# A block-sparse attention and MLP kernel: the fixed keys read by one wide product per head

## The chip, the cores and the metric

One core of a Trainium2 chip runs the whole program. The metric is the device time of one execution in microseconds (us). TensorE (PE) multiplies and writes to PSUM; VectorE (DVE), ScalarE (ACT) and GpSimd (POOL) do the rest of the arithmetic, and SyncE (SP), POOL and ACT issue DMAs.

## The reference

Attention over 4 batches, 8 heads, 768 positions of 64, in blocks of 32 (24 blocks). A query block sees the first and the last block, its neighbours (itself and one to each side), and three sampled blocks; the first and the last query block see everything. The output goes through an MLP with a squared ReLU (512 to 2048 to 512).

```python
mask = np.abs(blk_i - blk_j) <= window          # window = 1
mask = mask | (blk_i == 0) | (blk_j == 0) | (blk_i == n_blocks - 1) | (blk_j == n_blocks - 1)
for qb in range(n_blocks):
    for kb in sampled_blocks[qb]:
        mask[qb * block:(qb + 1) * block, kb * block:(kb + 1) * block] = True
scores = np.where(mask, scale * np.matmul(q, k.transpose(0, 1, 3, 2)), -1000000000.0)
attn = softmax(scores)                          # max, exp, sum + 1e-09
x = np.matmul(attn, v)                          # heads side by side: 3072 x 512
h = np.maximum(x @ w_in, 0.0)
return (h * h @ w_out)
```

## The kernel before

**Attention.** 128 query positions (4 blocks, index `j`) are a tile `t`; each batch `b` has 6, 24 in all, counted `k` in `order`. Half of the heads (4, as two pairs; `u` is the half, `i` the pair, `e` the head in the pair) of one tile is a `Half`, 48 in all. A pair's two heads lie on partitions 0 to 63 and 64 to 127. A Half's scores are two PSUM banks, one for each `e`; a pair takes 256 columns there: 64 for the two fixed blocks, 96 sampled, 96 neighbours (the window). Every block row `j` has its own sampled keys, so each product takes 32 queries: its shape on the array is 64 rows by 32 columns. Two products make a row of scores: one of 96 columns from `kn`, the batch's keys in block order, and one of 160 from `KG`, a tile into which the fixed keys are copied (four times, once for each `j`) beside the sampled ones. `static_keys` makes these copies, on POOL in the first batch and on ScalarE for the first two tiles of each later batch.

Then: maxima (DVE), exps (ACT), a turn of the probabilities (transposes `pt` on PE with copies `pT` in the first tiles; from tile 6 on ACT and DVE alone), and the values: per head and `j`, one product with V tile 0 (rows 0 to 63 the fixed blocks, 64 to 127 two sampled ones) and one with V tile 1 (rows 0 to 31 the third sampled block, 32 to 127 the window), 128 rows by 32 columns each, `pv`. `norm` divides. The first and last query blocks of a batch, which see everything, are four `Whole`s per batch (`g`, `pg`, `ptg`, `pvg`).

**MLP.** Three tiles make a chunk `c` of 384 positions, 8 chunks. `hidden` (`ph`) and `project` (`po`) each take three reduced-precision products for one exact one; in chunk 0 `project` uses plain fp32. Weights come raw from memory (`craw`) and are cut to fp32 by ACT and DVE (`cut`, `cut_bits`, `cut_split`), `AHEAD` steps behind the load. Attention of chunk c + 1 and later is woven into the MLP of chunk c by `Stream`, a list of generators with hand-set lags (`LAG`, `LAG_1`).

**The start.** Chunk 0's attention has no MLP to hide behind. Its four Wholes and six Halves begin `STEP_0` rounds apart, each with the lags of `LAG_0`. In it ACT also spreads the fixed values over the tiles (`copy_static`), ACT, POOL and DVE copy the windows of tiles 1 and 2 from `vn` (`copy_window`, one half of the heads at a time), and every `CUT_0[1]` rounds a weight cut begins. The SP queue brings tile 0's windows, then for each of the tiles 0, 1, 2 its twelve sampled blocks (`load_sampled`), whose addresses come from registers. Each engine works strictly in the order of the code.

Of the kernel before, what the change touches and what calls it, by code (L numbers as in the profile page):

```python
# [23 lines left out]
BLK = 32  # L24
# [29 lines left out]
AHEAD = 5  # L54
# [27 lines left out]
FIXED_0 = 7  # L82
ON_ACT = 12
# [13 lines left out]
def tile_block_sparse_attention_moe(ctx: ExitStack, tc, kd, knd, qd, qgd, vd, vnd, samp, const, wcat, out):  # L97
# [17 lines left out]
    def bank(name):  # L115
        return ps.tile([P, 512], F32, tag="s", name=name)

# [41 lines left out]
    KG = [one.tile([P, NJ, 2 + NRAND, NPAIR, BLK], F32, name=f"KG{i}") for i in range(2)]  # L159
# [12 lines left out]
    def load_keys(b, u, eng=nc.sync):  # L172

        kn = rot.tile([P, NBLK, 2, BLK], F32, tag=f"kn{u}", name=f"kn{b}_{u}", bufs=1)
        eng.dma_start(kn.rearrange("p a b c -> p (a b c)"), knd[b, u])
        st["kn", b, u] = kn
# [18 lines left out]
    def load_static(k, u, eng=nc.sync):  # L195
        us = halves(k, u)
        if us is None:
            return
        n = 1 if k == 0 else NJ
        for i in range(us.start, us.stop):  # L200
            src = columns(vd[order[k][0], V_STATIC * BLK :], i)
            src = src.unsqueeze(1).broadcast_to([2 * BLK, n, HW // 2])
            eng.dma_start(values_of(k)[0][0 : 2 * BLK, i, 0:n], src)

    def copy_static(k, i, copy):

        src = V[0][0][0 : 2 * BLK, i, 0:1]
        dst = V[k][0][0 : 2 * BLK, i, 1 if k == 0 else 0 :]
        copy(dst, src.broadcast_to(list(dst.shape)))  # L209

    def copy_window(k, i, j, n, copy):
# [5 lines left out]
        copy(V[k][1][(1 + n) * BLK : (2 + n) * BLK, i, j], st["vn", b, i][r : r + BLK, blk // NJ])  # L217

    def load_vn(b, hf, eng=nc.sync, own=None):

        vn = (own or rot).tile([P, NT, HW // 2], F32, tag="vn", name=f"vn{b}_{hf}", bufs=1)
        eng.dma_start(vn.rearrange("p t c -> p (t c)"), vnd[b, hf])
        st["vn", b, hf] = vn
# [15 lines left out]
    def load_q(b, t, eng=nc.sync, own=None):  # L239
        q = (own or rot).tile([P, NJ, NPAIR, BLK], F32, tag="q", name=f"q{b}_{t}", bufs=1 if own else 2)  # L240
# [4 lines left out]
    def keys_of(b, t, own):  # L245
# [3 lines left out]
            own.tile([P, NJ, 2 + NRAND, NPAIR, BLK], F32, name=f"KG{k}") if own else KG[(k - (k >= UC)) % 2]  # L249
# [3 lines left out]
    def copy_keys(b, t, own=None):  # L253

        vals = sampled(t, 0, POOL)
        kg = keys_of(b, t, own)
        for u in range(2):
            if t < UC:
                static_keys(b, t, u, nc.gpsimd.tensor_copy)
            kn = st["kn", b, u]  # L260
            for j in range(NJ):
                for r in range(NRAND):
                    nc.gpsimd.tensor_copy(
                        kg[:, j, 2 + r, 2 * u : 2 * u + 2].unsqueeze(1), kn[:, bass.ds(vals[NRAND * j + r], 1)]
# [5 lines left out]
    def load_kg(b, t):  # L270
# [3 lines left out]
        for j in range(NJ):  # L274
            for r in range(NRAND):
                nc.sync.dma_start(
                    kg[:, j, 2 + r].rearrange("p b c -> p (b c)").unsqueeze(1), k4[:, bass.ds(vals[NRAND * j + r], 1), :]
                )

    def static_keys(b, t, u, copy=nc.scalar.copy):  # L280

        src = st["kn", b, u][:, 0 : NBLK : NBLK - 1].rearrange("p i a c -> p i (a c)").unsqueeze(1)
        dst = st["kg", b, t][:, :, 0:2, 2 * u : 2 * u + 2].rearrange("p j i a c -> p j i (a c)")
        copy(dst, src.broadcast_to(list(dst.shape)))

    def load_window(k, u, eng=nc.sync):
        us = halves(k, u)
        if us is None:
            return
# [34 lines left out]
    class Half:  # L324
# [8 lines left out]
        def run(self, bank, lag):  # L333
# [9 lines left out]
            else:  # L343
                yield lag["x"]
                self.exps()
                self.next_keys()
# [12 lines left out]
        def scores(self):  # L359
# [3 lines left out]
            for i in range(2):  # L363
                pr = 2 * u + i
                for piece in range(2):
                    for j in range(NJ):
                        c = centre(NJ * t + j)
                        for e in range(2):
# [3 lines left out]
                            else:  # L372
                                k, a, z = kg[r, j, :, pr, :], 0, S_WIN
                            nc.tensor.matmul(  # L374
                                self.sb[e][j * BLK : (j + 1) * BLK, i * NSLOT + a : i * NSLOT + z],
                                q[r, j, pr, :],
# [21 lines left out]
        def next_keys(self):  # L398

            b, t = order[min(self.k + self.u, len(order) - 1)]  # L400
            if b > 0 and t < 2:
                static_keys(b, t, 1 - self.u)

        def turn_blocks(self):
# [4 lines left out]
            for j in range(NJ):  # L409
                if j == 2:  # L410
                    self.next_keys()
# [6 lines left out]
            nc.vector.transpose(self.pT.rearrange("p j h c q -> p (j h c q)"), p.rearrange("p j x s -> p (j x s)"))  # L418

# [20 lines left out]
        def copies(self, pt):  # L440
            self.pT = rot.tile([P, NJ, 4, 2, BLK], F32, tag="pT", name=f"pT{self.name}", bufs=2)
            for e in range(2):
                src = pt[e].rearrange("p (h j q) -> p h j q", h=4, j=NJ)
                dst = self.pT[:, :, 2 * e : 2 * e + 2].rearrange("p j i c q -> p (i c) j q")
# [5 lines left out]
        def values(self, bank):  # L450
            po = bank(f"pv{self.name}")
            for i in range(2):
                for e in range(2):
                    h = 2 * i + e
                    hv = h * VW
                    for c in range(2):
                        v = values_of(self.k)[c]
                        for j in range(NJ):
                            nc.tensor.matmul(  # L459
                                po[j * BLK : (j + 1) * BLK, h * VW : (h + 1) * VW],  # L460
                                self.pT[:, j, 2 * e + i, c],
# [544 lines left out]
```

## Time and profile before

| | us |
|---|---|
| median of 3 runs | 760.67 (758.05 to 761.56) |
| profiled execution | 760.55 |
| its span | 758.8 |
| PE busy | 732.4 (97%) |
| ACT busy | 539.7 (71%) |
| DVE busy | 499.8 (66%) |
| POOL busy | 502.3 (66%) |
| first MLP product (`ph`) begins at | 59.64 |

Spans on an engine are from start to modelled end; matmuls are pipelined, so neighbouring rows overlap, and the distance of two starts says what a row cost. An fp32 product has two records. In rows of PE, 64*32 behind the names is the part of the array used, rows by columns; 64x96 behind it the rows and columns that stream through.

### The profile page before, as it was taken

Reading aid. Unit: us, or ns where it says so; the run is one execution under the profiler, and the core shown is the slowest. Engines: PE = TensorE matmul, PEld = TensorE weight load, DVE = VectorE, ACT = ScalarE, POOL = GpSimd, SP = SyncE. Lnnn points to the kernel's source line nnn. Section 1 sums busy time; section 2 is a strip of 40 time slices with the busy share of each in tenths; the row PEclk is TensorE's granted clock in tenths of the full one; section 3 lists DMA queues with packets and bytes.
Section 4 is the critical chain, followed back from the end, with each engine's and each line's share of the span. In section 5 each row is a group of like instructions: output and inputs, shape, how many; then the busy total and the mean of one; then the engine's idle time right before and its main releaser. Section 6 shows DMA issues by size and latency. Waiting matters only on the chain.

```text
span 758.8 us, 26292 instructions
## 1 busy us (share of the span) xinstructions
PE 732.4 (97%) x9832; PEld 612.3 (81%) x9832; DVE 499.8 (66%) x987; ACT 539.7 (71%) x1193; POOL 502.3 (66%) x636
## 2 busy tenths in 40 slices
PE   4879999999999999999999999999999999999997
PEld 2656776668888888888888888887888888888986
DVE  5785785658785756667777575666868666645452
ACT  5896877798876876789786767679876776733222
POOL 6963844227776675757767567666876575777885
PEclk9799999999999999999999999999999999999999
DMA  8776799544543536544434344655344352201001
GB/s 283 224 215 172 228 264 344 130 117 131 140 114 93 146 86 176 153 109 128 113 105 106 101 126 109 221 120 140 79 124 118 75 143 64 51 1 44 1 1 41
DMA packets 92290, 97.45 MB, mean 128 GB/s; under 512 B 14787, under 2 KB 79428, under 8 KB 92164
## 3 DMA queue, kind: packets, MB, share of 16 engines
q1 hardware_dynamic: 86036, 72.41, 37.1%
q0 software_dynamic: 5696, 22.58, 9.2%
q8 instruction: 78, 1.28, 0.7%
q10 hardware_dynamic: 432, 0.79, 0.3%
q14 instruction: 48, 0.39, 0.2%
HBM read 89.43 MB, written 6.29 MB: 126 GB/s over the span
## 4 chain that ended last, share of the span: by engine, by line
PE 85%; ACT 5%; DMA 4%; DVE 4%; issue 1%; SPq 1%; ACTq 0%; POOL 0%; DVEq 0%; POOLq 0%
PE ph L788 33%; PE po L826 30%; PE s L374 7%; PE pv L459 5%; PE po L816 4%; PE g L546 2%; PE pvg L604 2%; DMA V<-in_v_dram 2%; DMA KG<-in_k_dram 1%; PE xt L773 1%; PE pt L437 1%; DVE xl L777 1%; ACT V L209 1%; DMA kn<-in_kn_dram 1%; SPq L317 1%
## 5 line engine op out<-in xcount | busy, mean ns | idle before, releaser
L413 ACT ACTIVATE pm<-p 32x256 f32<-32x256 f32 x576 | 239.2, 415 | 13.2 <-DVE p L391 4.8
L788 PE MATMUL ph<-xh,wi 128*128 128x384 f32 x832 | 237.8, 347 | 0.0
L826 PE MATMUL po<-wo,gh 128*128 128x512 f32 x672 | 213.8, 399 | 0.0
L755 POOL TENSOR_TENSOR wi<-W,wi 128x512 fp32r<-128x512 f32 x104 | 142.3, 1368 | 68.4 <-DVE wi L754 35.2
L806 POOL TENSOR_TENSOR gl<-gf,gh 128x384 fp32r<-128x384 f32 x112 | 117.4, 1048 | 93.0 <-DVE gf L804 80.6
L755 POOL TENSOR_TENSOR wo<-WO,wo 128x512 fp32r<-128x512 f32 x112 | 145.9, 1302 | 49.5 <-DVE wo L754 48.5
L792 ACT ACTIVATE r<-ph 128x384 f32<-128x384 f32 x128 | 63.0, 492 | 161.3 <-PE ph L788 156.1
L804 DVE SCALAR_TENSOR_TENSOR gf<-ph,r 128x384 f32<-128x384 f32 x112 | 62.3, 556 | 150.3 <-ACT r L792 136.4
L788 PEld LDWEIGHTS ph<-xh,wi 128*128 128x128 f32 x832 | 150.4, 188 | 13.4 <-issue 7.4
L826 PEld LDWEIGHTS po<-wo,gh 128*128 128x128 f32 x672 | 123.5, 188 | 23.0 <-issue 2.8
L788 PE MATMUL ph<-xl,wi 128*128 128x384 f32 x416 | 141.4, 340 | 0.0
L826 PE MATMUL po<-wo,gl 128*128 128x512 f32 x336 | 133.2, 396 | 0.0
L754 DVE CAST wo<-WO 128x512 fp32r<-128x512 f32 x112 | 84.4, 753 | 0.0
L788 PEld LDWEIGHTS ph<-xl,wi 128*128 128x128 f32 x416 | 78.2, 188 | 6.9 <-issue 2.9
L826 PEld LDWEIGHTS po<-wo,gl 128*128 128x128 f32 x336 | 63.1, 188 | 15.7 <-POOL gl L806 1.0
L385 DVE TENSOR_REDUCE m<-s 128x2 f32<-128x512 f32 x96 | 61.6, 683 | 11.2 <-PE s L374 10.9
L799 ACT ACTIVATE gh<-r 128x384 fp32r<-128x384 f32 x112 | 59.0, 526 | 9.3 <-ACT r L792 0.4
L459 PEld LDWEIGHTS pv<-V,pT 128*32 128x32 f32 x3072 | 47.7, 110 | 19.8 <-issue 9.5
L459 PE MATMUL pv<-V,pT 128*32 128x65 f32 x3072 | 56.2, 223 | 5.0 <-ACT pT L446 4.8
L788 PE MATMUL ph<-xh,WI 128*128 128x384 f32 x192 | 54.4, 344 | 0.8 <-ACT xh L776 0.8
L374 PE MATMUL s<-KG,q 64*32 64x160 f32 x1536 | 51.2, 305 | 1.4 <-issue 1.0
L418 DVE STREAM_TRANSPOSE pT<-pm 128x1024 f32<-128x1024 f32 x36 | 44.6, 1239 | 4.9 <-ACT pm L413 4.7
(85 smaller groups left out, 933.0 us busy)
## 6 DMA issues: line engine op xcount, KB each, us to landing
craw<-in_w_dram POOLq DMA_DIRECT2D x32, 512.0 KB, 5.9
V<-in_v_dram SPq DMA_DIRECT2D x504, 32.5 KB, 1.8
KG<-in_k_dram SPq DMA_DIRECT2D x216, 64.0 KB, 2.0
V<-in_v_dram SPq DMA_DIRECT2D x28, 390.0 KB, 4.5
q<-in_q_dram SPq DMA_DIRECT2D x24, 256.0 KB, 3.0
out_dram<-ot SPq DMA_DIRECT2D x21, 256.0 KB, 2.5
V<-in_v_dram SPq DMA_DIRECT2D x16, 292.5 KB, 4.2
vn<-in_vn_dram SPq DMA_DIRECT2D x5, 780.0 KB, 6.4
```

The lines of the kernel that those rows point to most:

```text
L374: nc.tensor.matmul(self.sb[e][j * BLK : (j + 1) * BLK, i * NSLOT + a : i * NSLOT + z], q[r, j, pr, :], k, start=True, stop=True,)
L385: nc.vector.tensor_reduce(m[:, e], self.sb[e].rearrange("p (i c) -> p i c", i=2), axis=AX, op=ALU.max)
L413: nc.scalar.activation(p[a * BLK : (a + 1) * BLK, j], x[j * BLK : (j + 1) * BLK, :, a], AF.Exp, scale=SCALE)
L459: nc.tensor.matmul(po[j * BLK : (j + 1) * BLK, h * VW : (h + 1) * VW], self.pT[:, j, 2 * e + i, c], v[:, self.u, j, hv : hv + VW], start=( ...
L754: nc.vector.tensor_copy(w[:, 0], src)
L755: nc.gpsimd.tensor_tensor(w[:, 1], src, w[:, 0], op=ALU.subtract)
L788: nc.tensor.matmul(ph[:, :TOK], w, x, start=(i == 0), stop=(i == len(steps) - 1))
L792: nc.scalar.activation(r, ph[:, :TOK], AF.Relu)
L799: nc.scalar.activation(gh, r, AF.Square)
L804: nc.vector.scalar_tensor_tensor(gf, ph[:, :TOK], 0.0, r, op0=ALU.max, op1=ALU.mult)
L806: nc.gpsimd.tensor_tensor(gl, gf, gh, op=ALU.subtract)
L826: nc.tensor.matmul(acc[c][u], g[:, at], w[:, k], start=(f == 0 and i == 0), stop=(f == NF - 1 and i == 2))
```

## The change

- **Scores, all batches.** Fixed keys aren't copied any more. For each pair and head, one product with all 128 queries of the tile (64 rows by 128 columns of the array) reads the first and last block of `KN` and gives the 64 fixed columns. The product with `KG` shrinks from 160 to 96 columns. The query's layout in memory and on chip is changed so that a pair's 128 queries are contiguous.
- **Values of the first three tiles.** The fixed blocks have one tile, `fixed`, for which each head has one product with 128 queries (64 rows by 128 columns); V tile 0 is then used from row 64 on (64 rows by 32 columns). Heads alternate in order so that equal shapes meet. `copy_static` is gone; tile 3 loads its fixed blocks four-fold from memory. `pv` and `pvg` of the first batch take their banks from the other PSUM pool.
- **Windows.** Tile 1's are copied for both halves at once, eight on POOL and four on ACT; tile 2's are loaded from memory, ahead of its sampled blocks on the SP queue.
- **Sampled keys of the first batch** are copied for both halves at once, but for tile 0.
- **Order of the start.** Half (0, 0) comes behind the second Whole, units begin 4 rounds apart instead of 5, with other lags; weight cuts are 4 steps behind their loads instead of 5.

```diff
-AHEAD = 5
+AHEAD = 4
-STEP_0 = 5
+N_0 = 1
+STEP_0 = 4
+FROM_MEMORY = (2,)
-LAG_0 = {"s": 2, "x": 2, "t": 3, "c": 2, "v0": 2, "n": 2}
+LAG_0 = {"s": 3, "x": 2, "t": 3, "c": 1, "v0": 3, "n": 2}
-FIXED_0 = 7
-ON_ACT = 12
+FIXED_0 = 22
+ON_POOL, ON_DVE = 8, 0
...
         def scores(self):
...
             for i in range(2):
                 pr = 2 * u + i
+                for e in range(2):
+                    r = slice(e * D, (e + 1) * D)
+                    to = self.sb[e][:, i * NSLOT : i * NSLOT + S_RAND]
+                    nc.tensor.matmul(to, q[r, pr].rearrange("p j s -> p (j s)"), kn[r, 0 : NBLK : NBLK - 1, i, :], start=True, stop=True)
                 for piece in range(2):
...
-                                k, a, z = kg[r, j, :, pr, :], 0, S_WIN
+                                k, a, z = kg[r, j, :, pr, :], S_RAND, S_WIN
...
+            for e, i, at in heads:
+                h = e, i, at
+                if e:
+                    self.products(po, h, 0, VA, 2 * BLK, True, False)
+                    self.products(po, h, 1, VB, 0, False, False)
+                p = self.pT[0 : 2 * BLK, 2 * e + i, 0].rearrange("p j q -> p (j q)")
+                nc.tensor.matmul(po[:, at], p, st["fixed"][:, self.u, at], start=e == 0, stop=e == 1)
+                if e == 0:
+                    self.products(po, h, 1, VB, 0, False, False)
+                    self.products(po, h, 0, VA, 2 * BLK, False, True)
...
-            return [(i * STEP_0, u) for i, u in enumerate(wholes + halves)]
+            whole = wholes[:2] + halves[:N_0] + wholes[2:] + halves[N_0:]
+            return [(i * STEP_0, u) for i, u in enumerate(whole)]
...
+    windows = [(copy_window, k, j, n) for k in range(1, UC) if k not in FROM_MEMORY for j in range(NJ) for n in range(3)]
+    for f, *at in windows[:ON_POOL]:
+        f(*at, nc.gpsimd.tensor_copy)
+    moves, fixed = windows[ON_POOL : ON_POOL + ON_DVE], windows[ON_POOL + ON_DVE :]
```

On PE, the first Half's scores (s) before, where they follow the Wholes' scores (g), values (pvg) and transposes (ptg):

```order
L546 MATMUL g_3_1_536<-kn_1_135,QG 128x256
L604 MATMUL pvg_1_540<-vn_0_133,pTg_1_528 32x65 x24
L584 MATMUL ptg_2_0_566<-ident,pg_2_531 128x128 x4
L584 MATMUL ptg_2_1_567<-ident,pg_2_531 128x128 x2
L374 MATMUL s_0_0_0_595<-kn_0_126,q_0_129 32x96
L374 MATMUL s_0_0_1_596<-kn_0_126,q_0_129 32x96
```

The same on PE in the change; the last two numbers are output partitions and columns, so 128x64 is the wide product:

```order
L581 MATMUL ptg_0_0_419<-ident,pg_0_411 128x128 x4
L581 MATMUL ptg_0_1_420<-ident,pg_0_411 128x128 x2
L353 MATMUL s_0_0_0_427<-KN,q_0_131 128x64
L353 MATMUL s_0_0_1_428<-KN,q_0_131 128x64
L363 MATMUL s_0_0_0_427<-KN,q_0_131 32x96
L363 MATMUL s_0_0_1_428<-KN,q_0_131 32x96
```

The scores begin with one wide product for each of the two heads (and do so again for the second pair), and the first Half's now follow the first Whole's transposes instead of the third's.

On PE, the end of the first Half's values before (pv, the second V tile last), with the transposes (pt) and scores behind it:

```order
L459 MATMUL pv_0_0_868<-V_78,pT_0_0_815 32x65 x4
L459 MATMUL pv_0_0_868<-V_79,pT_0_0_815 32x65 x4
L437 MATMUL pt_0_1_0_906<-ident,p_0_1_799 128x128 x4
L437 MATMUL pt_0_1_1_907<-ident,p_0_1_799 128x128 x4
L374 MATMUL s_1_1_0_984<-kn_1_135,q_1_143 32x96
```

On PE, the beginning of the same values in the change:

```order
L543 MATMUL g_3_0_569<-KN,QG 128x512
L543 MATMUL g_3_1_570<-KN,QG 128x256
L447 MATMUL pv_0_0_591<-fixed,pT_0_0_573 128x65
L457 MATMUL pv_0_0_591<-V_79,pT_0_0_573 32x65 x4
L457 MATMUL pv_0_0_591<-V_78,pT_0_0_573 32x65 x8
L457 MATMUL pv_0_0_591<-V_79,pT_0_0_573 32x65 x4
L447 MATMUL pv_0_0_591<-fixed,pT_0_0_573 128x65 x2
```

The first Half's values moved ahead of the third Whole's transposes, and three shapes take turns in them: fixed, V tile 1 (V_79), V tile 0 from row 64 (V_78).

On ACT, the beginning of the program before (pg are a Whole's exps, pTg its turned copy, L209 the fixed values, L217 the windows):

```order
L562 ACTIVATE pg_0_443<-g_0_0_434,mg_0_438 128x512
L562 ACTIVATE pg_0_443<-g_0_1_435,mg_0_438 128x256
L209 COPY V_78<-V_78 64x780 x2
L209 COPY V_122<-V_78 64x1040
L592 COPY pTg_0_466<-ptg_0_0_451 128x512
L562 ACTIVATE pg_1_469<-g_1_0_446,mg_1_459 128x512
L562 ACTIVATE pg_1_469<-g_1_1_447,mg_1_459 128x256
L209 COPY V_122<-V_78 64x1040
L209 COPY V_124<-V_78 64x1040 x2
L217 COPY V_125<-vn_0_133 32x260 x2
L592 COPY pTg_1_528<-ptg_1_0_504 128x512
```

On ACT, the same stretch in the change:

```order
L559 ACTIVATE pg_0_411<-g_0_0_398,mg_0_402 128x512
L559 ACTIVATE pg_0_411<-g_0_1_399,mg_0_402 128x256
L589 COPY pTg_0_465<-ptg_0_0_419 128x512
L559 ACTIVATE pg_1_468<-g_1_0_407,mg_1_414 128x512
L559 ACTIVATE pg_1_468<-g_1_1_408,mg_1_414 128x256
L589 COPY pTg_1_513<-ptg_1_0_501 128x512
L405 ACTIVATE p_0_0_474<-s_0_0_0_427,m_0_0_471 128x256 x2
L405 ACTIVATE p_0_0_474<-s_0_0_1_428,m_0_0_471 128x256 x2
L428 COPY pT_0_0_573<-pt_0_0_0_559 128x512
L428 COPY pT_0_0_573<-pt_0_0_1_560 128x512
L559 ACTIVATE pg_2_576<-g_2_0_509,mg_2_529 128x512
```

The copies of fixed values and windows are gone from it, and the first Half's exps (p) and copies (pT) stand ahead of the third Whole's exps.

More of the change, by code (lines that the diff above doesn't have):

```diff
@@ L158, in tile_block_sparse_attention_moe @@
     W1 = {f: one.tile([P, DM], F32, name=f"W1{f}") for f in SINGLE}
-    KG = [one.tile([P, NJ, 2 + NRAND, NPAIR, BLK], F32, name=f"KG{i}") for i in range(2)]
+    KN = one.tile([P, 2, NBLK, 2 * BLK], F32, name="KN")
+    KG = [one.tile([P, NJ, NRAND, NPAIR, BLK], F32, name=f"KG{i}") for i in range(2)]
     WO = {f: one.tile([P, DM], F32, name=f"WO{f}") for f in range(WO_LOW)}
@@ L195, in load_static, with copy_window @@
     def load_static(k, u, eng=nc.sync):
[L196 to L211, printed above, removed]
+        src = columns(vd[order[k][0], V_STATIC * BLK :], u)
+        src = src.unsqueeze(1).broadcast_to([2 * BLK, NJ, HW // 2])
+        eng.dma_start(values_of(k)[0][0 : 2 * BLK, u], src)
+    def copy_window(k, j, n, copy):
         b, t = order[k]
@@ L255, in copy_keys @@
         vals = sampled(t, 0, POOL)
[L256 to L260, printed above, removed]
+        k5 = keys_of(b, t, own).rearrange("p j r (u a) c -> p j r u (a c)", u=2)
+        for us in (slice(0, 1), slice(1, 2)) if t == 0 else (slice(0, 2),):
             for j in range(NJ):
@@ L396, in maxima @@
                 )
[L398 to L402, printed above, removed]
         def turn_blocks(self):
@@ L598, in values @@
             vn = st["vn", b, pr // 2]
-            po = bank(f"pvg{self.name}")
+            po = (ONE if self.b == 0 else bank)(f"pvg{self.name}")
             for kt in range(NT):
@@ L890, in tile_block_sparse_attention_moe @@
     load_q(0, 2, own=begin)
+    for k in FROM_MEMORY:
+        load_window(k, None)
     load_sampled(2, 1, nc.sync, SP)
-    windows = {
-        (k, u): [(copy_window, k, u, j, n) for j in range(NJ) for n in range(3)] for k in range(1, UC) for u in range(2)
-    }
     for k in range(2):
```

99 lines of the change are left out of this document (47 added, 52 removed).

## The prediction

> **What bounds the kernel now.** I read the page first (busy time, the slices), then the busy time by stage, then TensorE's rows in one steady stage and in the start.
>
> ```profile
> span 758.8 us, 26292 instructions
> PE 732.4 (97%) x9832; PEld 612.3 (81%) x9832; DVE 499.8 (66%) x987; ACT 539.7 (71%) x1193; POOL 502.3 (66%) x636
> ```
> ```profile
> 20.00:30.00 10.00, 7.80 (x270) 6.12 (x261) 7.53 (x24) 9.72 (x24) 9.44 (x26) 0.84 0.94 300
> 30.00:40.00 10.00, 8.93 (x238) 7.02 (x237) 8.52 (x24) 7.89 (x18) 10.00 (x42) 0.66 0.66 172
> 40.00:50.00 10.00, 7.90 (x320) 6.36 (x320) 8.27 (x17) 9.91 (x22) 2.83 (x9) 1.00 0.67 183
> 50.00:60.00 10.00, 6.82 (x169) 5.50 (x157) 7.89 (x20) 9.71 (x20) 7.53 (x25) 1.00 0.97 272
> 160.00:300.00 140.00, 140.00 (x2022) 118.76 (x2020) 98.03 (x197) 108.99 (x252) 94.49 (x95) 1.00 0.48 120
> ```
>
> Behind stretch and length each row has the busy time of TensorE, its weight loads, VectorE, ScalarE and GpSimd, then TensorE's granted clock, the DMA share and GB/s. There are two regimes. From about 60 us on TensorE is never free (140.00 of 140.00 at clock 1.00): there a microsecond that TensorE gains or loses is one of the whole, and what ScalarE, VectorE or GpSimd save is worth nothing. Up to 60 us ScalarE is the full one (9.71 to 9.91 of 10 in three of the four stretches), while TensorE has gaps. The change takes work from ScalarE in the start, and gives TensorE other work in both regimes. So the question is what TensorE pays.
>
> **The scores, where TensorE is full.** These are TensorE's rows around one half's values (pv) and scores (s) in mid-kernel; the tile after the operand names is rows*columns of the array, and an fp32 product has two records.
>
> ```profile
> 211.45 0.40 PE L826 MATMUL po<-wo,gl 128*128 128x512 f32 x1
> 211.78 0.89 PE L604 MATMUL pvg<-vn,pTg 128*32 128x65 f32 x48
> 212.59 0.73 PE L826 MATMUL po<-wo,gh 128*128 128x512 f32 x2
> 213.16 0.39 PE L826 MATMUL po<-wo,gl 128*128 128x512 f32 x1
> 213.39 0.63 PE L826 MATMUL po<-wo,gh 128*128 128x512 f32 x2
> ...
> 214.19 1.12 PE L459 MATMUL pv<-V,pT 128*32 128x65 f32 x64
> 215.23 0.40 PE L374 MATMUL s<-kn,q 64*32 64x96 f32 x16
> 215.42 0.48 PE L374 MATMUL s<-KG,q 64*32 64x160 f32 x16
> 215.69 0.37 PE L374 MATMUL s<-kn,q 64*32 64x96 f32 x16
> 215.86 0.58 PE L374 MATMUL s<-KG,q 64*32 64x160 f32 x16
> 216.37 0.44 PE L788 MATMUL ph<-xh,wi 128*128 128x384 f32 x1
> 216.65 0.34 PE L788 MATMUL ph<-xl,wi 128*128 128x384 f32 x1
> 216.83 0.51 PE L788 MATMUL ph<-xh,wi 128*128 128x384 f32 x2
> ```
>
> Read starts, not durations, which overlap. Sixteen KG records of 160 columns run from 215.42 to 215.69: 0.27 us, and eight tiles work side by side. Cutting 160 to 96 frees 0.27 x 64/160 = 0.108 per pair, 0.22 per half. The wide products put the same 64 columns through tiles of 64x128, of which only two (the two heads) fit side by side. One record of 160 columns takes 0.27/2 = 0.135 of its tile, so 64 take 0.054, two records 0.108, both heads together 0.108 per pair. That is what was freed: **as streaming, the exchange is even.** It can't gain.
>
> What is new is the change of tile shape in mid-stretch. What such a change costs stands in these rows. From pv (128*32) to s (64*32): 65 columns need 0.054 a record, 64 records four abreast 0.87, so pv's stream ends at 215.06 and s starts at 215.23: 0.17. From 128*128 to 128*32: one po record takes 0.23 (213.16 to 213.39), so the one of 211.45 ends at 211.68 and pvg starts at 211.78: 0.10. Back from 128*32 to 128*128: 48 records take 0.65, to 212.43, the next starts at 212.59: 0.16, and its first two take 0.57 against 0.47: 0.10 more for weights that weren't loaded ahead, 0.26 in all. From 64*32 to 128*128: 216.13 to 216.37 is 0.24, and 0.28 against 0.18 for the first record: 0.34. kn to KG, 64*32 both, costs nothing.
>
> Each half after the change goes wide, narrow, wide, narrow. Beside before, that is two changes to narrower columns, one back to wider, and wide weights at the entry. No row has 64*128, so the price is bounded: 0 if the two shapes share the array; at most 2 x 0.17 + 0.34 + 0.10 + 0.2 for weights of second records = 0.98. The nearest rows are those in which only the columns change: 2 x 0.10 + 0.26 + 0.10 = **0.56 us a half**, which I take. The halves of tiles 3 to 23 are computed while TensorE is full: 21 x 2 = 42. 42 x 0.56 = **+23.5 us** (0 to 41).
>
> The Trainium skill's page "TensorEngine Tiling (Array Packing)", Key Properties, speaks against the change: going to another tiling mode, not merely to another tile, empties the array first. The 0.17 and 0.26 agree; for 64x128 no run here shows it yet. By the rule the term is the 23.5, without it 0. Its page "TensorE: Matmul & The Clock Gate", LDWEIGHTS, has a weight load last as long as its columns, about 107 ns for 128. By that an estimate is that two loads a head, 0.21 a pair, outlast the streaming of 0.108, another 0.2 a half, and the whole would be 800.
>
> **The start.** The rows by ScalarE line from 10 to 60 us, the loads of tile 0's sampled values (all twelve, then the last two), and rows of the kinds that are counted below:
>
> ```profile
> L217 ACT COPY V<-vn 32x260 f32<-32x260 f32 x24 | 9.7, 406 | 0.4
> L423 ACT ACTIVATE p<-s,m 128x256 f32<-128x256 f32 x24 | 9.7, 530 | 0.1
> L446 ACT COPY pT<-pt 128x512 f32<-128x512 f32 x12 | 7.0, 662 | 2.0 <-PE pt L437 1.9
> L209 ACT COPY V<-V 64x1040 f32<-64x1040 f32 (+1 forms) x6 | 5.5, 987 | 0.0
> L710 ACT ACTIVATE craw<-craw,below 128x512 int32<-128x512 uint16 x6 | 5.2, 873 | 0.0
> L562 ACT ACTIVATE pg<-g,mg 128x512 f32<-128x512 f32 (+1 forms) x8 | 4.2, 578 | 8.4 <-DVE mg L555 8.4
> ```
> ```profile
> L317 SPq DMA_DIRECT2D V<-in_v_dram x12: 569/570/702, 8.2 to 20.7; - x12
> ...
> DMA to landing us min/median/max: 2.2/5.3/9.8
> ```
> ```profile
> L317 SPq DMA_DIRECT2D V<-in_v_dram x2: 569/570/570, 20.0 to 20.7; - x2
> ...
> DMA to landing us min/median/max: 4.8/5.3/5.9
> ```
> ```profile
> 24.83 0.87 PE L584 MATMUL ptg<-ident,pg 128*128 128x128 f32 x6
> ...
> 34.94 1.96 PE L459 MATMUL pv<-V,pT 128*32 128x65 f32 x64
> ...
> 53.97 1.09 PE L437 MATMUL pt<-ident,p 128*128 128x128 f32 x8
> ...
> 55.21 1.25 ACT L446 COPY pT<-pt 128x512 f32<-128x512 f32 x2
> ...
> 57.34 1.53 PE L773 MATMUL xt<-ident,x 128*128 128x128 f32 x12
> 59.64 0.44 PE L788 MATMUL ph<-xh,WI 128*128 128x384 f32 x1 [0.78 <-ACT xh L776]
> ```
>
> ScalarE loses the six static value copies (5.5) and 24 window copies (9.7), gets four window copies of twice the width (about 0.6 each, between L217's 0.41 and L209's 0.99: 2.4) and one weight cut fewer (about 1.6): 14.4 us less. That would be the gain, were ScalarE still last. Two things take its place.
>
> First, the values of half (0,0) move up in TensorE's order, from behind all four Wholes to behind two. In the chain g, exps, ptg, s, exps, pt, copies they could start near 20 us. But they read the sampled values of tile 0, the twelve loads whose last is issued at 20.7 and lands 5.9 later, at **26.6**; before, they began at 34.94 and never waited. The change leaves those twelve on the SP queue behind the same loads (one fewer). Everything on TensorE behind this product waits too: ptg of Wholes 2 and 3, all later scores; and behind them ScalarE's copies.
>
> Second, TensorE itself. A half's values were 1.04 in steady rows. Now the fixed blocks have a product of their own per head (64 rows x 128 columns, 65 through: 0.108, four times 0.43), and shapes go 64*128, 128*32, 64*32, 128*32 and back twice: 3 x 0.17 + 0.26 = 0.77, twice 1.54. 1.04 + 0.43 + 1.54 = 3.0 (1.5 to 3.5). Scores are 1.14 (215.23 to 216.37) + 0.56 = 1.7. From 26.6 the order holds six pv (18.0), five s (8.5), five pt (5.4), two ptg (1.7), two pvg (1.8): 35.4. In the last two halves nothing lies between pt and pv, so the copies are waited for: 2 x 1.25. From the last pv's end to the first ph before: 57.34 to 59.64, 2.3. Sum 26.6 + 35.4 + 2.5 + 2.3 = 66.8, against 59.64: **+7.2 us**. Per half ScalarE needs 1.62 of exps and 1.17 of copies (9.7 and 7.0 over six) and 1.6 for a cut (0.87 and its like), 4.4 against TensorE's 5.8, so it is covered. If shapes are free, pv is 1.5 and ScalarE is last: behind the first pv it has two pTg copies (1.2), one Whole's exps (1.05), the window copies (2.4), a cast (0.7) and five times 4.4: 27.3; the last cut (1.6) doesn't delay. Then 26.6 + pv 1.5 + ptg 0.9 + 25.7 + pv 1.5 + 2.3 = 58.5: -1.1. Low end: besides that the last load lands 2.2 after issue, at 22.9: -4.8. High: +10, and more if the granted clock falls to the 0.66 of 30 to 40 us.
>
> **The rest.** The static key copies, six on GpSimd in the start and twelve on ScalarE under the full TensorE, and merged key copies: 0, since both engines have room there (GpSimd waits for tile 0's keys and is ready before the first scores). Tile 2's windows by DMA (0.8 MB), and four-fold static values of tile 3 (0.4 MB more): 1.2 MB at 270 GB/s are 4.4 us of transfers, at 40 to 50 us, where the DMA share is 0.67; tile 2's sampled loads move about 1 us later, and its values come far later than that. Without this cover 1 to 2 us. One step less of lead for raw weights: 0 to 2, taken as 0. The flat layouts of q and pT: 0. The bank that pv takes elsewhere frees pt: at most one pT copy, within the low end.
>
> Sum: 760.55 (this execution, 758.8 of span; the median is 760.67) + 23.5 + 7.2 = **791 us**.
>
> **Rivals.** (1) *Shapes share the array.* Then scores cost 0 and the start -1.1, giving 759.4. For it: tiles of one shape do run eight abreast. Against it: every change of shape in these rows has a gap. (2) *Faster*: the same, and the sampled values land at 22.9, since the first raw weights are asked for at another time: 755.7. It decides only if a half's scores pay under 0.05 us, since 42 x 0.05 is 2. (3) *Half price*: only the return to wide costs, 0.26 a half: +11, start +2: 773.
>
> **Numbers.** A difference under 0.5% (3.8 us) can't be told from none. Forecast 0.65 (775 to 808: from 0.36 a half, 15 in all, and no loss in the start, to 0.9 a half and +10); half price 0.09, slower too; shapes free and no change 0.09; faster 0.17. So slower 0.74, same 0.09, faster 0.17. The range must reach past rival 1 to hold 8 in 10: 757 to 808.
>
> **What would show it.** Right: gaps of 0.1 to 0.3 in TensorE's starts around each 64*128 row, and about 1.7 from a half's first score to the next ph; span in the full stage longer by 0.5 to 0.6 a half; the first pv waiting for a DMA near 26 us; the first ph near 67. Wrong: a stretch of 1.14 as before, or a first ph before 58. The forecast fails if 64*128 and 64*32 follow each other without a gap.

## The result, and the profile after

The change makes the kernel slower: 801.4 us (median of 4 runs, 798.07 to 805.04) against 759.79 (4 runs, 758.05 to 761.56), a ratio of 1.054 with a 95% interval of 1.050 to 1.059. The runs of the changed kernel differ with their mean granted clock (0.972 to 0.985); the profiled one is the longest, 805.04, with a span of 803.3. So its span grew by 44.5, from 758.8. Two kernels below, the one without the early half and the one with the filled wait, had one execution of four in a slower state, over 1.5% above their fastest, and their times are those of the other three.

The busy time by stage of the changed kernel, with the columns as before (stretch, length, TensorE, its weight loads, VectorE, ScalarE, GpSimd, TensorE's granted clock, DMA share, GB/s):

```profile
20.00:30.00 10.00, 2.84 (x36) 1.76 (x37) 1.44 (x4) 0.25 (x1) 7.79 (x21) 0.69 0.87 273
30.00:40.00 10.00, 10.00 (x172) 7.61 (x171) 3.08 (x8) 4.39 (x8) 2.89 (x12) 0.50 0.70 170
40.00:50.00 10.00, 10.00 (x284) 7.90 (x284) 7.00 (x23) 5.96 (x15) 3.88 (x14) 0.96 0.53 123
50.00:60.00 10.00, 8.18 (x217) 6.15 (x222) 3.75 (x9) 7.46 (x17) 0.41 (x1) 0.90 0.70 175
60.00:70.00 10.00, 10.00 (x142) 7.34 (x126) 4.81 (x10) 3.29 (x8) 2.43 (x4) 0.50 0.88 239
70.00:80.00 10.00, 10.00 (x121) 7.51 (x121) 2.82 (x8) 2.94 (x5) 0.00 (x0) 0.50 0.24 58
160.00:300.00 140.00, 140.00 (x1848) 114.24 (x1847) 94.58 (x188) 107.98 (x247) 81.84 (x90) 1.00 0.47 120
```

In the start the bound has moved. ScalarE, full before (9.7 to 9.9 of 10), now has room everywhere; TensorE stands idle from 20 to 28 us but for a few products, and from then on it is the full engine, but for some 36 us at half clock. In the full stage nothing is idle, as before. TensorE's rows in the start (duration behind the start; in brackets the idle time ahead and what ended it) say how long the start became:

```profile
19.87 0.40 PE L447 MATMUL pv<-fixed,pT 64*128 64x65 f32 x2
20.20 0.51 PE L457 MATMUL pv<-V,pT 128*32 128x65 f32 x4
26.02 0.43 PE L457 MATMUL pv<-V,pT 128*32 128x65 f32 x2 [5.31 <-DMA V<-in_v_dram]
28.30 1.39 PE L457 MATMUL pv<-V,pT 128*32 128x65 f32 x26 [1.85 <-DMA V<-in_v_dram]
...
45.71 0.43 PE L447 MATMUL pv<-fixed,pT 64*128 64x65 f32 x2
...
48.75 1.09 PE L419 MATMUL pt<-ident,p 128*128 128x128 f32 x8
...
58.11 0.38 PE L363 MATMUL s<-KN,q 64*32 64x96 f32 x4 [1.82 <-issue]
...
60.34 0.68 PE L447 MATMUL pv<-fixed,pT 64*128 64x65 f32 x2
...
65.29 1.97 PE L419 MATMUL pt<-ident,p 128*128 128x128 f32 x8
...
82.48 0.45 PE L786 MATMUL ph<-xh,WI 128*128 128x384 f32 x1 [0.67 <-ACT xh L774]
```

The first MLP product comes at 82.48 instead of 59.64: 22.8 us of the 44.5. The other 21.7 lie behind it. One half in mid-kernel:

```profile
227.21 1.12 PE L457 MATMUL pv<-V,pT 128*32 128x65 f32 x64
228.25 0.44 PE L353 MATMUL s<-KN,q 64*128 64x64 f32 x4
228.62 0.40 PE L363 MATMUL s<-KN,q 64*32 64x96 f32 x16
228.81 0.37 PE L363 MATMUL s<-KG,q 64*32 64x96 f32 x16
229.11 0.44 PE L353 MATMUL s<-KN,q 64*128 64x64 f32 x4
229.48 0.40 PE L363 MATMUL s<-KN,q 64*32 64x96 f32 x16
229.67 0.37 PE L363 MATMUL s<-KG,q 64*32 64x96 f32 x16
229.97 0.45 PE L786 MATMUL ph<-xh,wi 128*128 128x384 f32 x1
```

From the first score to the next product it takes 1.72 us (228.25 to 229.97), where it took 1.14. All halves between 100 and 700 us have this as their median.

### The profile page after: what moved, and what is told of

Its sections match the earlier page's. It is cut to its first block, busy times and chain, and to the rows that moved or that the text cites. A ratio compares the mean times of both kernels' runs of the same rounds, so it can differ in the third digit from the quotient of the medians.

```text
span 803.3 us, 26982 instructions
## 1 busy us (share of the span) xinstructions
PE 782.0 (97%) x10264; PEld 648.1 (81%) x10264; DVE 494.4 (62%) x975; ACT 520.0 (65%) x1155; POOL 484.0 (60%) x566
## 4 chain that ended last, share of the span: by engine, by line
PE 92%; DMA 2%; DVE 2%; ACT 1%; SPq 1%; issue 1%; POOL 0%; ACTq 0%; POOLq 0%; DVEq 0%
PE ph L786 33%; PE po L824 28%; PE pv L457 7%; PE s L363 6%; PE po L814 5%; PE s L353 4%; PE g L543 2%; DMA q<-in_q_dram 2%; PE pt L419 2%; PE pvg L601 2%; PE pv L447 1%; PE xt L771 1%; DMA V<-in_v_dram 1%; DVE xl L775 1%; PE ptg L581 0%
## 5 line engine op out<-in xcount | busy, mean ns | idle before, releaser
L752 DVE CAST wo<-WO 128x512 fp32r<-128x512 f32 x112 | 81.6, 729 | 0.0
L457 PE MATMUL pv<-V,pT 128*32 128x65 f32 (+1 forms) x3072 | 62.8, 229 | 7.2 <-DMA V<-in_v_dram 7.2
L457 PEld LDWEIGHTS pv<-V,pT 128*32 128x32 f32 (+1 forms) x3072 | 49.3, 112 | 24.9 <-issue 11.8
L380 DVE TENSOR_TENSOR p<-s,m 128x512 f32<-128x512 f32 x72 | 46.0, 680 | 0.1
```

What stands on the lines that cost most here:

```text
L457: nc.tensor.matmul(po[j * BLK : (j + 1) * BLK, at], self.pT[r:, 2 * e + i, c, j], v[r:, self.u, j, at], start=start, stop=stop,)
L752: nc.vector.tensor_copy(w[:, 0], src)
```

## Experiments: the scores

The theory T: every change of tile shape costs TensorE time, and the start is a loss of its own. Its rival R1: it is the loading of weights 128 columns wide that costs.

**The scores alone** (the kernel before, with the wide product and the query layout; `KG` without fixed keys):

```diff
+                for e in range(2):
+                    to = self.sb[e][:, i * NSLOT : i * NSLOT + S_RAND]
+                    nc.tensor.matmul(to, q[r, pr]..., kn[r, 0 : NBLK : NBLK - 1, i, :], start=True, stop=True)
-                                k, a, z = kg[r, j, :, pr, :], 0, S_WIN
+                                k, a, z = kg[r, j, :, pr, :], S_RAND, S_WIN
```

> The kernel before with the change to the scores alone (wide product for the fixed keys, no copies of fixed keys, the query layout of the change); the values, the windows and the order of the start stay as before. Theory T (each change of tile shape costs TensorE time; the start is a separate loss): 1.72 instead of 1.14 from a half's first score to what follows, in 42 halves +24.4 us, and +0 to +4 in the start's six halves: 783 to 789 us, ratio 1.031 to 1.038, and the first ph between 60 and 64 us. Rival (the whole 41 us come from one cause that is not the shapes, such as a lower clock all through): then a steady half takes 1.14 here and the time is within 1% of before, 753 to 768.

Measured: 782.85 us (781.13 to 789.41), ratio 1.029 (1.025 to 1.034), 1.72 us in a half, and the first ph here:

```profile
62.14 0.44 PE L787 MATMUL ph<-xh,WI 128*128 128x384 f32 x1 [0.72 <-ACT xh L775]
```

So the scores alone explain the steady loss and 2.5 us of the start: about half of the whole. It fell just below the range expected (783 to 789), since behind the first ph the span grew by 19.7 (781.0 - 62.14 against 758.8 - 59.64), not by 24.4. Part of the difference is waits of the kernel before that went: between 100 and 700 us TensorE had 2.8 us of gaps there (for ScalarE's exps pg and keys KG, and one of 1.04 with no reason shown), and has none here; the other 1.9 us are not traced.

**Both pairs' wide products first** (the change with one wide stretch in a half instead of two):

```diff
             for i in range(2):
                 pr = 2 * u + i
                 for e in range(2):
                     ...wide product...
+            for i in range(2):
+                pr = 2 * u + i
                 for piece in range(2):
```

> The change, with the wide products of both pairs of a half ahead of its narrow ones: the same products, but wide, narrow instead of wide, narrow, wide, narrow. Theory T (a price for each change of shape): one return to the wide shape (0.14) and one step back to the narrow one (about 0.15) fall away in each half, so 1.42 instead of 1.72 and 0.29 x 48 = 14 us less than the change: ratio to before 1.033 to 1.039. Rival R1 (what costs is the loading of wide weights, eight records a half wherever they stand): at most 2 us less than the change, ratio to before 1.05 to 1.056.

**Wide products of half the width** (two of 64 rows by 64 columns for each of 64x128):

```diff
-                    to = self.sb[e][:, i * NSLOT : i * NSLOT + S_RAND]
-                    nc.tensor.matmul(to, q[r, pr]..., start=True, stop=True)
+                    to = self.sb[e][hw * 64 : (hw + 1) * 64, i * NSLOT : i * NSLOT + S_RAND]
+                    nc.tensor.matmul(to, q[r, pr, 2 * hw : 2 * hw + 2]..., start=True, stop=True)
```

> The change, with each wide product of 64 rows by 128 columns cut into two of 64 rows by 64 columns, which lie side by side. Theory T (the price is for leaving and entering a shape, however wide it is): within 6 us of the change, 1.6 to 1.75 in a steady half, ratio to before 1.045 to 1.057. Rival R1 (the price is the loading of weights 128 columns wide): the load is halved, 1.4 to 1.5 in a half, 10 to 15 us less than the change, ratio 1.035 to 1.04.

Measured: with the wide products first 798.06 us (792.07 to 799.37), ratio 1.046 (1.042 to 1.051), 1.52 in a half (median of 40); with half the width 794.67 (790.42 to 800.65), ratio 1.044 (1.038 to 1.049), 1.53 in a half. Their medians lie 3 and 7 us below that of the change, with intervals that touch its own or nearly do. In both profiles the start was no shorter than the change's (first ph at 83.39 and 83.56, clock at 0.50 from 67 to 90 us), so the gain in the full stage hardly shows in the whole, and the rows decide. One wide stretch in the first kernel:

```profile
228.15 0.66 PE L353 MATMUL s<-KN,q 64*128 64x64 f32 x8
228.74 0.40 PE L365 MATMUL s<-KN,q 64*32 64x96 f32 x16
```

and in the second:

```profile
228.71 0.34 PE L355 MATMUL s<-KN,q 64*64 64x64 f32 x8
228.99 0.40 PE L365 MATMUL s<-KN,q 64*32 64x96 f32 x16
```

Four wide records took 0.37 (228.25 to 228.62), eight in a row take 0.59: four more cost 0.22. That is 0.11 for each of the two records of a head, with both heads side by side, while their streaming needs 0.054. So of the 0.37, 0.22 go with the records and 0.15 with leaving the shape. At half the width it is 0.28, 0.09 less: the 0.22 go with the width of the weights, not with the columns that stream, which are the same. Neither theory was right alone: dropping one round trip gives 0.20 where T said 0.29 and R1 almost nothing; halving the width gives 0.19 where T said none and R1 0.2 to 0.3. Of the 0.20, 0.15 are the wide products themselves (0.59 against 2 x 0.37) and only 0.05 the narrow ones with the way to the next product (0.93, 228.74 to 229.67, against 2 x 0.49). The Trainium skill's page "TensorE: Matmul & The Clock Gate", section on LDWEIGHTS, has a load of 128 columns last about 107 ns; the 0.11 a record agrees. The rows of the weight loads themselves last longer, with medians of 184 ns for 64x128, 132 for 64x64 and 105 for 64x32 in these profiles, and so grow by some 0.8 ns with each column, 0.105 us for 128: the part that grows is the 0.11, and that the rest is hidden behind other work is not shown.

**No wide product** (the change, with the fixed keys read from `KN` by a product of 32 queries per j, ahead of the two others; no copies either):

> The change, with the fixed keys still read from KN, without copies, but by one product of 32 queries for each j (64 rows by 32 columns), like the other scores; no wide product in the scores. Theory T: one shape, so a half takes 1.14 to 1.2 again, 24 us less than the change in the steady stretch, and some 3 less in the start: 772 to 780 us, ratio 1.018 to 1.028; what remains is the start, with the first ph still near 75 to 82. Rival R3 (more products in a half cost by their number, 16 records of 64 columns instead of 4): a half stays at 1.5 or more, and the time within 10 us of the change.

Measured: 802.95 us (800.88 to 806.08), ratio 1.054 (1.051 to 1.058): nothing gained, and T's 772 to 780 missed. The time is where R3 put it, but not for R3's reason, a half of 1.5 or more: a half has a median of 1.24, near what T said, but a mean of 1.68 over the 42 halves behind the first ph, against 1.77 in the change. The views of waits and of DMA queues (packets, MB, share) of this kernel show what took its place:

```profile
PE s L361 <- issue: 13.4, 9, 3.9
...
PE pv L455 <- DMA V<-in_v_dram: 4.9, 2, 2.6
PE pt L417 <- issue: 3.4, 2, 2.0
```
```profile
q8 instruction: 91, 1.49, 0.8%
```

"issue" is idle time for which the profile shows no reason: 13.4 us in nine gaps ahead of scores, up to 3.9 in one, where the change had one gap of 1.8. The kernel has 2304 instructions more than the change (29286 against 26982), and its instruction queue moved 91 blocks where the change's moved 82, nine more, 256 instructions each. The Trainium skill's page "Runtime: NRT & Kernel Launch", section "Instruction fetch mechanics", says that instructions come in blocks of 256, which agrees, and that their loading is mostly hidden, which does not hold here if the gaps are waits for it.

**More products in the kernel before** tells whether the number of products does this by itself (the product of 160 columns from `KG` cut into 64 and 96, same columns, same tiles):

```diff
-                for piece in range(2):
+                for piece in range(3):
+                            elif piece == 1:
+                                k, a, z = kg[r, j, 0:2, pr, :], 0, S_RAND
                             else:
-                                k, a, z = kg[r, j, :, pr, :], 0, S_WIN
+                                k, a, z = kg[r, j, 2:, pr, :], S_RAND, S_WIN
```

> The kernel before with the product of 160 columns from KG cut into two of 64 and 96, all 64 rows by 32 columns: the same columns and the same tiles, 16 products more in each half, 768 in all. Theory I (TensorE can't be given so many short instructions; in the kernel with narrow products for the fixed keys a half took 1.24 instead of 1.14, and 15.5 us of gaps without a shown reason came between 100 and 700 us): 1.24 in a half, 8 to 16 us of such gaps, 770 to 780 us, ratio 1.013 to 1.026. Rival (those gaps came from other parts of the change): only the 0.1 a half, 763 to 766, ratio 1.004 to 1.008.

Measured: 778.95 us (776.69 to 783.48), ratio 1.025 (1.020 to 1.030), 1.30 in a half, and these waits:

```profile
PE s L376 <- issue: 9.2, 6, 4.0
...
PE pv L461 <- issue: 5.7, 3, 2.3
...
PE po L828 <- issue: 1.7, 2, 1.2
```

The time is as theory I had it, with more in a half (1.30 for 1.24) and more gaps (17 us for 8 to 16) than it said: 16 products more in a half, without any new column or shape, cost 18 us, through 0.16 a half and some 17 us of unexplained gaps (2.7 in the kernel before), 11.9 of them in the start (first ph at 66.95). The waits of values for ScalarE's copies pT fell meanwhile from 4.8 to 1.4 us, so the gaps cost less than they last. It also says what the wide product was good for: it keeps the number of instructions down (8 records more in a half than before, where narrow products take 32). That the gaps are waits for instructions fits the blocks, but no row names them; this is argued, not shown.

## Experiments: the start

Theory W: the wait for the sampled values and the half clock behind it are the loss. Theory V: the values in three shapes are.

**Half (0, 0) behind all four Wholes** (`-N_0 = 1`, `+N_0 = 0`):

> The change with N_0 = 0: half (0,0) comes behind all four Wholes again, all else as in the change. In the change TensorE stood for 7.2 us in that half's values, waiting for the sampled values of tile 0 (18.4 to 28.3 us), and the clock was 0.50 from 23 to 40.5. Theory W (the wait, and the low clock behind it, are the start's loss): the wait goes and the work of 28 to 40 runs at 1.00, so the first ph comes 7 to 13 us earlier than 82.5, at 69 to 75, and the time is 788 to 795 us, ratio 1.036 to 1.045. Rival V (the added work of the values, 3.0 us a half and twice that at clock 0.50, is the loss, and the order matters little): first ph 79 to 83, time within 4 us of the change, ratio 1.05 to 1.056.

**Values as before** (six copies of the fixed blocks on ScalarE, two products of 128x32 per head and j):

```diff
-FIXED_0 = 22
+FIXED_0 = 7
...
-            if self.k >= UC:
+            if True:
                 for h in heads:
                     self.products(po, h, 0, VA, 0, True, False)
...
+    fixed = [(copy_static, k, i) for k in range(UC) for i in range(2)] + fixed
```

> The change with the values of the first three tiles as in the kernel before: the fixed blocks are copied into V tile 0 by six copies on ScalarE (about 0.99 each, from the fixed tile), and values have two products per head and j, all 128 rows by 32 columns; scores, windows and order stay as in the change. Theory V (three shapes in turn in the values are the start's loss): 1.04 instead of 3.0 at full clock and 1.9 instead of 4.95 at half, six times, 12 to 18 us of TensorE; first ph at 64 to 70 us, time 783 to 789, ratio 1.028 to 1.037. Rival W (the wait for sampled values, and the low clock behind it, are the loss): first ph at 76 or later, at most 6 us gained, ratio 1.046 or more.

Measured: without the early half 787.67 us (787.56 to 793.98), ratio 1.040 (1.032 to 1.048); with the old values 786.44 (784.10 to 787.56), ratio 1.034 (1.029 to 1.040). The first ph in the one and in the other:

```profile
65.48 0.44 PE L786 MATMUL ph<-xh,WI 128*128 128x384 f32 x1 [0.67 <-ACT xh L774]
```
```profile
62.27 0.44 PE L791 MATMUL ph<-xh,WI 128*128 128x384 f32 x1 [0.68 <-ACT xh L779]
```

Both ratios lie where the theory that each was to test had put them, but both first phs came earlier than those theories said (69 to 75 and 64 to 70). Each edit, alone, takes back 17 to 20 of the start's 22.8 us in the profiled executions, and 13.7 and 15.0 us of the whole in the medians; the profiled execution of the change is its slowest. So neither is "the" cause; something multiplies them. In the first kernel the values still cost 3.0 each, their first wide product stands at 32.59 instead of 19.87, and the start is shorter all the same. Its clock:

```profile
20.00:30.00 10.00, 6.21 (x187) 5.02 (x180) 5.70 (x19) 4.54 (x9) 9.61 (x28) 0.87 0.86 271
30.00:40.00 10.00, 10.00 (x267) 7.54 (x265) 4.38 (x12) 6.26 (x14) 2.53 (x12) 0.96 0.59 152
40.00:50.00 10.00, 10.00 (x270) 7.63 (x269) 4.92 (x13) 5.92 (x15) 2.36 (x8) 1.00 0.85 220
50.00:60.00 10.00, 9.41 (x196) 7.08 (x194) 6.95 (x15) 7.78 (x17) 3.35 (x4) 1.00 0.91 267
```

0.87 to 1.00 where the change had 0.50 to 0.96.

**Filled wait** (dense products into the bank of the first values, while they wait):

```diff
+            if self.k == 0 and self.u == 0:
+                for _ in range(FILL):   # 34
+                    nc.tensor.matmul(po[:, 0 : 4 * VW], ident, KN[:, 0]...[:, 0 : 4 * VW], start=True, stop=True)
```

> The change with 34 products of 128 rows by 128 columns, 260 columns streamed, added ahead of half (0,0)'s values; they write the bank that the values then overwrite, and only keep TensorE busy through the wait for the sampled values (34 times about 0.23 us is 8 us, 20 to 28 us). Theory C (the idle wait lowers the clock to 0.50, and the 12 us of work up to 40 us are paid twice for it): clock 1.00 from 20 to 40, first ph about 6 us earlier than 82.5, at 75 to 78, time 793 to 797, ratio 1.042 to 1.048; the second fall, behind the gap of 1.8 us at 56 to 58, may come all the same. Rival (the clock falls with the kind of work that follows, not with idleness): 0.50 from about 30 on as before, first ph at 82 to 84, time within 2 us of the change or up to 2 above it.

Measured in the profiled execution, TensorE's rows and one window over the whole rest of the start:

```profile
20.07 15.14 PE L444 MATMUL pv<-KN,ident 128*128 128x260 f32 x68
35.14 0.43 PE L451 MATMUL pv<-fixed,pT 64*128 64x65 f32 x2
...
74.86 0.44 PE L790 MATMUL ph<-xh,WI 128*128 128x384 f32 x1 [0.78 <-ACT xh L778]
```
```profile
20.00:74.80 54.80, 52.37 (x1021) 41.21 (x1020) 23.35 (x63) 25.98 (x55) 18.37 (x51) 1.00 0.67 191
```

The filler was twice as long as meant (0.22 is a record, and a product has two), so the values began 6.8 us later than in the change, at 35.14. Yet the first ph came 7.6 us earlier, and the clock was 1.00 throughout, as theory C had it. From the values' start to the first ph it is 39.7 us here and 54.2 in the change (28.30 to 82.48), with the same work in the same order, of which the change had 8 records done by then: the half clock, with the gap at 58 us, is worth some 14.5 us. The timed median, which C had put at 793 to 797, hardly shows it: 799.65 us (796.39, 799.65 and 805.75 at mean clocks of 0.998, 0.996 and 0.980), ratio 1.055 (1.047 to 1.063). The filler takes its own time in every execution, and the clock was not as high in all.

**A dense block in the half-clock stretch** (8 such products ahead of the values of half (1, 1)):

> The change with 8 dense products (128 rows by 128 columns, 260 columns streamed, 16 records; 0.22 us a record at full clock, 0.44 at half) ahead of the values of half (1,1), in the middle of the stretch from 58 to 80 us that ran at clock 0.50 without a gap; they write the bank that the values overwrite. Theory S (the low clock lasts because the values in three shapes keep the array too sparsely busy; dense work ends it): the clock goes to 1.00 within 7 us of the block's start and stays there to the first ph; the block costs 4 to 7 us, the 14 us behind it are halved, so first ph 79 to 83 and a time within 4 us of the change. Rival L (the low clock lasts for a time of its own, whatever runs): 0.50 up to about 80 us, the block costs its full 7 us, first ph at 88 to 90, time 5 to 8 us above the change. If no gap lowers the clock near 57 us in the profiled execution, neither is told.

Measured: 799.04 us (797.57 to 804.23), ratio 1.049 (1.045 to 1.054). The block, and the clock ahead of and behind it:

```profile
63.73 5.21 PE L444 MATMUL pv<-KN,ident 128*128 128x260 f32 x16
68.87 0.43 PE L451 MATMUL pv<-fixed,pT 64*128 64x65 f32 x2
...
83.08 0.45 PE L790 MATMUL ph<-xh,WI 128*128 128x384 f32 x1 [0.78 <-ACT xh L778]
```
```profile
50.00:60.00 10.00, 10.00 (x155) 7.48 (x154) 4.36 (x10) 3.84 (x8) 0.00 (x0) 0.50 0.70 190
60.00:66.00 6.00, 6.00 (x82) 4.45 (x81) 2.08 (x4) 4.34 (x9) 1.21 (x1) 0.50 0.63 141
67.00:83.00 16.00, 14.71 (x253) 11.16 (x251) 6.14 (x16) 7.63 (x16) 0.64 (x2) 1.00 0.31 106
```

What theory S expected came: ahead of the block TensorE was "busy" 16.00 of 16 us and had 0.50; about 3 us into the block the clock was at 1.00 and stayed there to the first ph, which with 5.2 us of added work came 0.6 later (83.08 against 82.48). Scores, transposes and values in three shapes kept the row of busy time full here without bringing the clock back. But the test had asked for a fall by a gap near 57 us, and in this execution the clock fell near 49 us with no gap over 0.36 us in the 10 us ahead. And low stretches also end without such a block, the first of the change at 40.9 us behind a Whole's values and transposes. So that the block ended this one is supported by its timing in one execution, and not shown.

The lengths say more. In all thirteen profiles, up to 110 us, every stretch at 0.50 lasted a multiple of 3.4 us, read from windows of half a microsecond: 3.4, 6.8, 10.2, 13.7, 17.1, 20.5, 23.8 or 34.1. It looks as if the clock were set once in 3.4 us by what TensorE did in them. Here the last 3.4 us ahead of the fall, 46.2 to 49.6, are nearly all values of one half in three shapes (46.35 to 49.39), and the last ahead of the return, 63.3 to 66.7, nearly all dense block (from 63.73). This fits S; no run tests it.

**Two tries at a gain.** Tile 2's windows from memory, in the kernel before and alone:

```diff
+    load_window(2, 1)
     load_sampled(2, 1, nc.sync, SP)
-    fixed += windows[2, 0] + windows[2, 1][:ON_ACT]
-    moves = windows[1, 1] + windows[2, 1][ON_ACT:]
+    moves = windows[1, 1]
```

> The kernel before with one part of the change: tile 2's windows are loaded from memory (ahead of its sampled blocks on the SP queue) instead of copied, tile 1's stay on GpSimd and VectorE; scores, values, lags and order as before. ScalarE loses 24 copies, 9.7 us, in the start. Theory A (in the start before, TensorE waits for ScalarE, 9.9 us in all up to 60 us, so relief of ScalarE is worth time there): first ph at 54 to 58 us instead of 59.64, time 754 to 759, ratio 0.991 to 0.998. Rival B (the transfers that take the copies' place, 0.8 MB more on the SP queue, delay tile 2's sampled values, or TensorE waits for something else): first ph within 1 us of 59.64 or later, ratio 0.998 to 1.004.

Measured: 763.19 us (758.92 to 768.30, 12 runs), ratio 1.005 (1.001 to 1.008). Rival B; the first ph is later, not earlier:

```profile
45.02 1.51 PE L459 MATMUL pv<-V,pT 128*32 128x65 f32 x43 [4.37 <-issue]
53.60 0.32 PE L459 MATMUL pv<-V,pT 128*32 128x65 f32 x8 [0.90 <-DMA V<-in_v_dram]
55.45 1.72 PE L459 MATMUL pv<-V,pT 128*32 128x65 f32 x50 [1.52 <-DMA V<-in_v_dram]
62.57 0.44 PE L788 MATMUL ph<-xh,WI 128*128 128x384 f32 x1 [0.78 <-ACT xh L776]
```

The values' waits for ScalarE's copies pT did shrink, from 4.8 us to 0.6, but others took their place: values waited 2.4 us for tile 2's blocks, and an unexplained gap of 4.4 came at 40 to 45 us, while the DMA share, as the view gives it, was 1.10.

Dense products in the waits of the kernel before:

```diff
             po = bank(f"pvg{self.name}")
+            if b == 0:
+                for _ in range(FILL[pr]):   # 2, 5, 0, 1
+                    nc.tensor.matmul(po[:, 0 : 4 * VW], ident, QG..., start=True, stop=True)
```

> The kernel before with dense products ahead of a Whole's values, where TensorE waited anyway: 2, 5, 0 and 1 of them (0.44 us each) ahead of the values of the four Wholes of the first batch; they write the bank that the values overwrite. In the profile before, TensorE waited there for 1.0, 2.3, 0 and 1.0 us, and the clock was 0.50 from 20 to 23.5 and from 30 to 37. Theory C (idle gaps of 2 us lower the clock): the first low stretch goes, worth 1.7 us; the second, behind a gap of 1.7 us in which TensorE waited for nothing that the profile shows, may stay; 754 to 759 us, ratio 0.992 to 0.999, faster by 0.5% only if both go. Rival (the fillers delay what they precede): 760 to 764, ratio 1.0 to 1.006.

Measured: 759.35 us (757.69 to 765.77, 12 runs), ratio 0.999 (0.996 to 1.002): no difference that can be told. The row of 20 to 24 us has a clock of 1.00 where the kernel before has 0.60:

```profile
20.00:24.00 4.00, 3.17 (x140) 2.50 (x130) 3.41 (x11) 3.88 (x9) 3.84 (x9) 1.00 0.77 225
```

but the gap at 28 to 30 us stayed (2.58), the fall behind it too, and the first ph came at 59.48. No version beat the kernel before.

## Why the prediction was right, and where it was off

The direction and the forecast case were right, 801.4 us within 757 to 808, 10 above the 791 predicted. The range reached down to no change at all, so the rows say more than the time does.

- **Scores, +23.5: right in size by some luck, wrong inside.** 0.58 a half against 0.56. The parts differ, and their errors nearly cancel: the exchange is not "even as streaming", because two wide records of a head take 0.22 by their loading and not 0.108; the changes of shape cost less than taken, 0.15 out of the wide one, 0.14 back into it by the rows (where one such way back was left out, only 0.05 came off), nothing at the entry from pv (1.04 from pv to the first score in both kernels), and the exit to ph is 0.10 cheaper. By stretches: 2 x 0.37, +0.03 and +0.02 in the narrow ones of the first and second pair, -0.21 in the last: 0.58. The estimate of 0.2 a half for weight loads, which stood in a sentence by itself, was one of the true parts, though with it the forecast would have been 0.76 a half. 42 x 0.58 is 24.4, and 21.7 came; the waits of 2.8 us that went, and that the sum didn't count, are of that size.
- **The wait of the first values: right.** Asked for at 19.87 (said: near 20), ended at 28.30 by the loads of sampled values (said: 26.6).
- **Values 3.0, scores 1.7: right** at full clock: 45.71 to 48.75 is 3.04. At half clock it is 4.95 (60.34 to 65.29).
- **The start, +7.2: mis-sized; this is the step that failed.** The work from the wait's end to the first ph was put at 40.2 us (66.8 - 26.6), and took 39.7 where the clock was 1.00 throughout. In the change it took 54.2. The 15.7 us too little are 1.7 of the later landing, 14.5 of the clock and of the gap at 58, less 0.5. The text named this case ("and more if the granted clock falls to the 0.66") as an end of the range and gave it no price. It should have: the sum itself put an idle wait of 7 us into TensorE's start, and the profile before showed 0.66 behind a gap.
- **The rest, 0: not contradicted.** The window copies that left ScalarE gained nothing in the kernel before, as the run with windows alone shows; the static copies had no run of their own there. In that run the first ph came 2.9 us later, more than the 1 to 2 put for the transfers without cover; in the change no wait for tile 2's values is among the rows.
- **Rivals.** Shapes that share the array, and half the price, are excluded by the 1.72 in a half; the faster case rested on the first of them.

Open: what TensorE waits for in the "issue" gaps, what measure of TensorE's work the clock follows, and so whether a block of dense work would end a low stretch each time.

## What to carry to other kernels

Before merging small products into a wide one, price it as the load of its weights plus the way out of and back into its shape, not as its columns; and before splitting instead, count the instructions, since 768 short ones more cost 18 us here. An idle wait ahead of sparse work can cost more than itself: price the work behind it at half clock too, as an end of the range, for in the change that lasted for 17 and 24 us.

## What the runs showed of the hardware that was not expected

- The granted clock stayed at 0.50 for about 24 us (58 to 82) while TensorE's busy time was full; once it returned about 3 us into 16 dense records.
- Its low stretches up to 110 us all lasted multiples of 3.4 us.
- It fell behind a gap of 1.8 us (58.11), and once with none over 0.36 in the 10 us ahead.
- 768 short products more, with the same columns and tiles, cost 18 us.
